# A two-layer transformer on one core: the first loads in another order and other pieces, with the order of work laid out anew

## The chip, the cores and the metric

The kernel runs on one core of a Trainium2 chip. The metric is device time of one execution in microseconds (us). The kernel before takes 2652.07 us, the median of three runs (2652.02 to 2653.28).

## The reference, cut to what matters

```python
def _A_ref(x, mem0, Wq, Wk, Wv, Wo, seg_len):       # x 2048 x 576; 32 heads of 128; memory of 8 rows
    mem = mem0
    for s in range(64):                             # segments of 32 rows, one after the other
        h = jnp.concatenate([mem, x[:, s * 32:(s + 1) * 32, :]], axis=1)        # 40 rows
        q, k, v = (jnp.einsum('btd,dhe->bhte', h, W) for W in (Wq, Wk, Wv))
        scores = jnp.einsum('bhqe,bhke->bhqk', q, k) * scale
        p = _softmax(jnp.where(mask[None, None], scores, -1000000000.0), axis=-1)
        o = jnp.einsum('bhte,hed->btd', jnp.einsum('bhqk,bhke->bhqe', p, v), Wo)
        mem = o[:, :8, :].copy()                    # the next segment needs this one's output
        outs.append(o[:, 8:, :])
def _B_ref(x, w1, w3, w2):                          # 576 -> 4608 -> 576
    return jnp.einsum('bsf,fd->bsd', _silu(x @ w1) * (x @ w3), w2)
x = x + _A_ref(_layernorm(x), ...); x = x + _B_ref(_layernorm(x), ...)
x = x + _A_ref(_layernorm(x), ...); x = x + _B_ref(_layernorm(x), ...)          # the same weights again
```

All inputs and weights are bf16. A segment depends on the one before it through `mem`.

## The kernel before, in words

The kernel walks through 72 steps. Step t works on segment t of the first attention layer and, from step 8 on, on segment t - 8 of the second one as well: steps 0 to 7 and the last eight have one layer, those between have two. Attention runs in a step by four groups of eight heads; the feed-forward part runs in jobs, one for every four steps, beside the attention of later steps.

The work is cut into nodes. `make_nodes` (L236) makes them with costs, dependencies and the pools they take room from; `plan` (L80) walks through them in the order of estimated times and lets each engine record its instructions in that order. Every engine keeps the order that the plan gives it. The order on TensorE is not found by the plan: it is written out by hand in three strings, `FIRST` (L205), `FOUR` (L214) and `LAST` (L218). `ORDER = FIRST + FOUR * 11 + LAST`, so `FIRST` is 16 steps, `FOUR` four steps that are walked through eleven times, and `LAST` the last twelve. One letter is one node:

- `Q`, `q`: queries and keys of four heads, the four full chunks of the 576 rows of Wq and Wk, and the remainder of 64 rows. A `Q` is 32 matmuls, a `q` eight. There are eight of each in a step.
- `S`: scores of a group; then VectorE and ScalarE make the softmax into tile `PB`. `T`: transposes of it on TensorE, in steps of one layer. In steps of two layers a transposing DMA takes `PB` to `PTS` instead (node TRD).
- `V v X x G g`: values, `P`: probabilities times values (it reads `PTS` and `V`), `O`, `o`: the product with Wo, full chunks and remainder.
- `F f`: w1 and w3 of 256 of the 4608 columns, `W w`: the product with w2 for the first and the second layer. `a b n m p`: transposes around the layernorms.

A node has a mode: which part of the array its matmuls use (whole, halves of columns, halves of rows). Some nodes can run whole or by halves; then `plan` takes what the nodes beside them have, and by halves such a node has twice the instructions (`Emitter.mm`). Which of ACT and DVE empties a bank is also the plan's choice (nodes "AD").

Loads: `em.dma` issues on SyncE's queue (SP), `em.adma` on ScalarE's (ACT), `em.swdma` on GpSimd's. Costs and due times of a load only set where it stands in its queue; on the chip an instruction waits for the data it reads or overwrites and, in the queue of a DMA, for one of eight semaphores that the DMAs of SP and ACT take in turn. Before, the loads go like this: SP has the 64-row remainder of Wq and half of that of Wv, then the first half of the heads of Wq in four pieces of 512 KB (one for each 128 rows) and of Wk in four, then the second half in eight, then Wv in four pieces of 1 MB, Wo in four groups, w1 and w3 of the first feed-forward nodes, w2, and x of the second 128 rows. ACT has the remainder of Wk, x of the first 128 rows, mem0, and the other half of Wv's remainder.

In step 0 the first `Q` of each half of the heads is preceded by twelve matmuls with no use of their result (L920 to L922), three behind each chunk of Wk as it lands:

```python
for c in range(4 if first and t == 0 and u % 4 == 0 else 0):
    for _ in range(3):
        self.mm(self.bk(b[1])[:], self.T.ident[:, 0:P], self.T.W[:, 4 + c, u * 512:(u + 1) * 512], True, True)
```

`first` is true if this `Q` stands ahead of the `q` of the same four heads. Ahead of everything, L1303 to L1321 fill constants: GpSimd does the masks, `HT` and `YTS`, VectorE `PB`, `V` and the eight banks.

Of the kernel before, what the change touches and what calls it, by code (L numbers as in the profile page):

```python
# [13 lines left out]
P = 128  # L14
R64 = 64
D = 576
# [183 lines left out]
def ewh(*ns):  # L200
# [5 lines left out]
    "maQQQqqqqQSQQTSqQQqSTqqSvVXxPPTOPOTOooPoOoQqqqqQQSQQSqvVQqQSqTQqXPSTOPTOaooPxTOPoOoQqqQQSQqqvVqSQqqQQqSTQPSTOPOT"  # L206
    "PTOPoooOoQqqqqQQSQvVSqqQQqqQQSTPTSXPOoTxPTOPOOoooQqqqpQQvVSqnQQqfSFQQqqqQSTFfTSPFOfPoTWPOFTOPfooOoFQQqqqfQSFfqqV"
    "vQWSQQFqfqTQSFWqfPQOTFPSfXWoTxfOPTFPOOoooFfqqQQFSQfqVvqqQWSQTFfqfFQQPSWTQfqqOPSFTOPFWTOPooffOooFQQqqqqQSQWVvSFfq"
    "QQTqWqqSQPTQaOSPbOTXPxooTOPxoOoXpqqQQqqQSQqvnQSfFQqVSfqFQfFPqQfFSPWfFPOoOOoofFPWOoFQQqfqfFSQqqqqQQQSWGSqqgQQFfgP"
    "GSWPGFfggfFGPOOWPOOooooFfqqQQQfSFqqQvFSWVfqqQQfFSWqQQqfPPSFOOFoPWOffFPaooOoWQqqqqQQSbQQSGgqqqQQgSPGqQOSPGOgGPgoO"  # L210
    "PooOoQqqqppQQQvSqqVnnSQFqqfQQFPSqffQFPOSoWwFFPffOOWPwOoooFqffqQQFwQQqqfSWGFSFqgqfQQQPQSWFqfqgGSwggGPGOPOOPWOFooo"
    "oFffqqQQQQqqawSSFfqqqQQQWvSwVffqFQFPPWSwFfOOPFWwffFPOOooooWQQqqqQSqqqQQQSbwGSgqqgQQPGSggGPGOPOOPoooOo"
)
FOUR = (  # L214
    "QqqqppQvVSQQnnQFfqqFSfqqQQFfqQSwPWPSFffOOWPFwFPOOooooFffqqQQwQQqqgSWGSFqqfQQQPQSWFqfqfFSwGgggGPGOPOPOOwoooFWoFff"
    "qqQQQQqqSFSqqfQQwWvVSQQFfqqfFSPWPOOwFffPFOWPwOooooFqqfQQqqaSQQWqSQQqqqQQSbwGSggGPGPggGPOOOPoooOo"
)
LAST = (  # L218
    "QpqqqQpQSvqqQQnSVqQnQFPSffqqFQOPSFOwPooffOFPWOooFqfqqQQQQfqSWwGSgqFQFPQwQqqfGSFfqgQOPSWggGGPOFPOOoWowooFfqfqQQQQ"
    "qqSWFSfqqQQwVvFSFfqqfQQPWOPSwFoOoffFPwPOOoWoFfqqqQQQQSWwqfFSFfqqQQWvvVSVqqPQQOSbwXPxPOOPoooOoQQpqqpVvqqQSQQqSnnQ"  # L220
    "QqqFTSffqFPTQOPSWFffTFPTOOPwOooooFfqqQQQSQQvqqqVwFWSfqfFqqQQQTSwWSFPTffOTPFOTPwPOOooooWFfqfqFQQQSQqqvxXVwWSFTFff"
    "qqQQQwqqSQTPWPffSFOTFPwTOPOWOooooFvfqqVQQWSFQqfqQwSFfqqQQqTSqWQPTQOTSPPoOObwTxoPXOooQQqqvpSQQqqVSnqQFfqQFTSQfqPQ"
    "qfTFSPOTwFPOOTFPffooOoowVqqqvQQQSQfqqFSQQqqqwQSTQPFTSOPXffOTFPTxOPwOooooFFqqffQQqqQSQQSqqVvqfQFTSQwPQqfTOSFPFTOf"
    "PwTOPFOfooooQQqqqQSvqqQVSqQTQSPQQqqTOSPFwTFffPOTOPoooOopwfFnFfffFFwFwfffFFFwffFFwfffFFwFwfffFFFwffFFwfffFFww"
# [11 lines left out]
def make_nodes(em, nseg, pools, o=Opt, dma_bw=230e3, load_bw=400e3):  # L236
# [26 lines left out]
    node("DMA", 4.0, lambda n: None, prio=-999.0, name="boot")  # L263
    ld_m0 = node("ACT", 0.6, em.load_m0(), prio=-90, name="m0", lat=8.0)
# [97 lines left out]
    def step(t):  # L362
# [17 lines left out]
        for g in range(NG):  # L380
            qs, qe = [], []
            for u in (2 * g, 2 * g + 1):
# [3 lines left out]
                m_ = node("PE", 32 * mm80, em.qk(t, u, b), deps=hx + hm[:1] + ([ld_h[u // 4]] if t == 0 else []),  # L386
                          prio=pq, mode="full", acq=[q] + b, name="QK")
                n = node("PE", 4 * mm80, em.qk_tail(t, u, b), deps=hx + hm + ([ld_h[u // 4]] if t == 0 else []), prio=pq + o.qkt, mode="row",
# [75 lines left out]

    last_up = []
    last_reads = [], []
    kept = {}

    def job(j):

# [113 lines left out]
class Emitter:  # L584
# [83 lines left out]
    def load_qk(self, half):  # L668
        def f(n):
            h = slice(half * 2048, (half + 1) * 2048)  # L670
# [690 lines left out]
```

## Time and profile before

| | before |
|---|---|
| median of three runs | 2652.07 us |
| the profiled execution / its span | 2657.81 us / 2656.0 us |
| busy: PE, DVE, ACT, POOL | 97%, 76%, 48%, 5% of the span |
| TensorE's granted clock, mean | 0.995 |
| instructions | 131716 |
| DMA | 373.13 MB, 140 GB/s in the mean |

The profiled execution's own time is 1.8 us over its span, and 5.7 us over the median. Lines name the place in the kernel file; nearly all matmuls have line L607 (`Emitter.ch` records them), so groups are told apart by their tiles and shapes. In a row of matmuls, 128*64 means that 128 rows and 64 columns of the array are in use.

### The profile page before, as it was taken

The numbers are of one execution on the slowest core, as the hardware profiler recorded it, in microseconds if no ns is written. First come the engines' busy times: TensorE is split into PE (matmuls) and PEld (weight loads), VectorE is DVE, ScalarE is ACT, GpSimd is POOL, SyncE is SP. The second block draws the span as 40 slices with busy tenths as digits, with TensorE's granted clock in tenths as the row PEclk, the third lists the DMA queues.
The fourth block names the chain that finished last, engine by engine and source line by source line (L and its number), as shares of the span: only waits on it lengthen the run. The fifth ranks groups of instructions, "written<-read, shape, count | busy, mean of one in ns | idle before, by whom it ended". The sixth has DMA issues, their size and how long they took to land.

```text
span 2656.0 us, 131716 instructions
## 1 busy us (share of the span) xinstructions
PE 2579.5 (97%) x58546; PEld 2209.3 (83%) x58546; DVE 2011.5 (76%) x5145; ACT 1265.5 (48%) x3744; POOL 128.8 (5%) x182
## 2 busy tenths in 40 slices
PE   6999999999999999999999999999999999999998
PEld 4788888788888878888888888888888888888886
DVE  4777786787787778778877777877777777777876
ACT  2655554444445444444545444454544445444552
POOL 1000000000000000000000000000000000000000
PEclk8999999999999999999999999999999999999999
DMA  9065745565555546446455654545465464545467
GB/s 322 4 181 136 185 105 145 121 154 133 126 143 112 148 118 157 131 130 146 114 142 114 157 133 128 147 111 140 117 158 147 119 155 93 142 120 148 118 172 247
DMA packets 686027, 373.13 MB, mean 140 GB/s; under 512 B 233897, under 2 KB 675633, under 8 KB 684817
## 3 DMA queue, kind: packets, MB, share of 16 engines
q1 hardware_dynamic: 681920, 356.84, 51.9%
q8 instruction: 457, 7.49, 1.2%
q0 software_dynamic: 3024, 6.93, 0.9%
q10 hardware_dynamic: 512, 0.94, 0.1%
q14 instruction: 114, 0.93, 0.1%
HBM read 308.49 MB, written 2.36 MB: 117 GB/s over the span
## 4 chain that ended last, share of the span: by engine, by line
PE 85%; DMA 8%; DVE 3%; issue 1%; SPq 1%; ACT 1%; POOL 0%; ACTq 0%; DVEq 0%; POOLq 0%
PE bank L607 85%; DMA PTS<-PB 5%; DMA W<-in_B_w_dram 2%; SPq L616 1%; DVE PB L613 1%; DMA W<-in_A_Wk_dram 1%; DMA W2C<-in_B_w_dram 1%; DVE STAT L613 0%; DVE SME L613 0%; DVE HTT L613 0%; DMA XN<-in_A_x_dram 0%; ACT V L610 0%; ACT HT L610 0%; DVE XR L613 0%; ACT SME L610 0%
## 5 line engine op out<-in xcount | busy, mean ns | idle before, releaser
L607 PEld LDWEIGHTS <-W 128*128 128x128 bf16 (+2 forms) x32064 | 1250.8, 100 | 129.4 <-issue 70.6
L607 PE MATMUL bank<-HT,W 128*128 128x80 bf16 (+3 forms) x23040 | 791.4, 197 | 13.9 <-issue 7.2
L607 PE MATMUL bank<-XTB,W 128*64 128x256 bf16 (+5 forms) x9024 | 662.5, 263 | 8.6 <-DMA W<-in_B_w_dram 5.5
L610 ACT ACTIVATE QKT<-bank 128x64 bf16<-128x64 f32 (+2 forms) x1645 | 377.4, 309 | 282.5 <-PE bank L607 270.8
L607 PE MATMUL bank<-OT,WO 128*128 128x80 bf16 (+2 forms) x11520 | 401.3, 198 | 3.7 <-issue 1.7
L610 ACT ACTIVATE V<-bank 32x512 bf16<-32x512 f32 (+1 forms) x577 | 324.9, 584 | 161.5 <-PE bank L607 155.4
L607 PEld LDWEIGHTS <-WO 128*128 128x128 bf16 (+1 forms) x11520 | 376.2, 102 | 24.9 <-issue 12.8
L607 PE MATMUL bank<-WV,HT 128*32 128x512 bf16 (+5 forms) x3592 | 366.7, 384 | 0.7 <-issue 0.7
L607 PE MATMUL bank<-W2C,HTT 128*64 128x288 bf16 (+1 forms) x3208 | 324.4, 287 | 1.0 <-DMA W2C<-in_B_w_dram 1.0
L613 DVE TENSOR_TENSOR PB<-SME,STAT 40x128 bf16<-40x128 f32 (+4 forms) x912 | 275.6, 336 | 40.0 <-DMA PTS<-PB 30.8
L610 ACT ACTIVATE HTT<-bank 128x512 bf16<-128x512 f32 (+1 forms) x324 | 175.0, 550 | 265.0 <-PE bank L607 263.1
L613 DVE TENSOR_REDUCE STAT<-SME 104x8 f32<-104x320 f32 (+1 forms) x576 | 275.2, 478 | 15.5 <-ACT SME L610 7.4
L613 DVE SCALAR_TENSOR_TENSOR XR<-bank,XR 128x288 f32<-128x288 f32 x576 | 240.5, 447 | 59.5 <-PE bank L607 54.7
L607 PEld LDWEIGHTS <-HT 128*32 128x32 bf16 (+5 forms) x3592 | 152.2, 99 | 145.8 <-issue 40.3
L610 ACT ACTIVATE OT<-bank 128x320 bf16<-128x320 f32 (+1 forms) x430 | 157.9, 403 | 229.4 <-PE bank L607 224.5
L613 DVE SCALAR_TENSOR_TENSOR HTT<-HTT,bank 128x512 bf16<-128x512 bf16 (+1 forms) x324 | 202.0, 624 | 80.0 <-ACT HTT L610 76.9
L607 PEld LDWEIGHTS <-HTT 128*64 128x64 bf16 (+1 forms) x3272 | 233.7, 105 | 30.9 <-issue 2.8
L613 DVE TENSOR_TENSOR HTT<-HTT,bank 128x512 bf16<-128x512 bf16 (+1 forms) x324 | 203.6, 628 | 29.5 <-PE bank L607 1.4
L610 ACT ACTIVATE SME<-SME 104x320 f32<-104x320 f32 (+1 forms) x288 | 135.6, 471 | 172.3 <-DVE SME L613 169.7
L613 DVE CAST V<-bank 64x512 bf16<-64x512 f32 (+1 forms) x287 | 196.1, 686 | 20.7 <-PE bank L607 14.8
L613 DVE CAST QKT<-bank 128x128 bf16<-128x128 f32 (+4 forms) x403 | 108.4, 316 | 100.0 <-PE bank L607 98.3
L613 DVE TENSOR_TENSOR SME<-bank,maskb 104x320 f32<-104x320 f32 (+1 forms) x288 | 138.4, 481 | 35.0 <-PE bank L607 29.1
(58 smaller groups left out, 1332.7 us busy)
## 6 DMA issues: line engine op xcount, KB each, us to landing
W<-in_B_w_dram SPq DMA_DIRECT2D x612, 256.0 KB, 3.6
W2C<-in_B_w_dram SPq DMA_DIRECT2D x306, 288.0 KB, 3.4
W<-in_B_w_dram SPq DMA_DIRECT2D x612, 32.0 KB, 3.5
W<-in_B_w_dram SPq DMA_DIRECT2D x8, 1024.0 KB, 13.6
W<-in_A_Wq_dram SPq DMA_DIRECT2D x9, 512.0 KB, 8.5
WO<-in_A_Wo_dram SPq DMA_DIRECT2D x4, 1152.0 KB, 16.7
XR<-in_A_x_dram POOLq DMA_DIRECT2D x16, 288.0 KB, 3.8
WV<-in_B_w_dram SPq DMA_DIRECT2D x4, 1152.0 KB, 10.0
```

The lines of the kernel that those rows point to most:

```text
L607: self.ch("PE", self.nc.tensor.matmul(out, lhsT=lhsT, rhs=rhs, start=start, stop=stop, skip_group_check=True, **k))
L610: self.ch("ACT", self.nc.scalar.activation(*a, **k))
L613: self.ch("DVE", getattr(self.nc.vector, fn_)(*a, **k))
L616: self.ch("SP", self.nc.sync.dma_start(out=out, in_=in_))
```

## The change

Loads: x of the first 128 rows and mem0 stand first, on ACT's queue; the four 64-row remainders (Wq, Wk, twice Wv) follow there. SP starts with Wq and Wk by quarters of the heads: 1 MB of Wq and 1 MB of Wk, four times, each one DMA over all four chunks of rows, with lines of 2 KB where they were 4 KB. The rest of SP's order stays, except that the first two w2 loads stand behind both of the first w1 and w3 loads. The nodes of these first feed-forward loads get a dependency on `WO2` of step 0 in the plan. In the built program that is only a place in the queue: these loads wait for semaphores of earlier DMAs there, and for none of TensorE's, before and after.

Useless matmuls: asked for ahead of `Q` 0, 2, 4 and 6 if they come ahead of their `q`, reading zeros in `V` and not the chunks of Wk. With the new string that is so for `Q` 6 alone: 24 such matmuls become 12.

Constants: `PB` and `V` are filled by GpSimd and not by VectorE.

Plan: other costs for the first loads, and all three strings are new, with the same letters in another order. The built programs have 58546 matmuls before and 58759 after, and 1198 and 1182 changes of mode.

```diff
-def make_nodes(em, nseg, pools, o=Opt, dma_bw=230e3, load_bw=400e3):
+def make_nodes(em, nseg, pools, o=Opt, dma_bw=230e3, load_bw=395e3):
...
-    ld_t = [load("ldt", 1.7 * kb(3 * R64, 4096), -10.0, em.load_tails(0)), node("ACT", 0.6, em.load_tails(1), prio=-120, name="ldt", lat=8.0)]
-    node("ACT", 0.6, em.load_tails(2), prio=-80, name="ldt", lat=10.0)
-    ld_h = [load("ldqk", kb(512, 4096), half - 9.0, em.load_qk(half)) for half in (0, 1)]
+    ld_t = [node("ACT", 0.6, em.load_tails(i), prio=-100 + i, name="ldt", lat=10.0) for i in range(4)]
+    ld_h = [load("ldqk", kb(1024, 1024) + (kb(3 * R64, 4096) if i == 0 else 0), i - 19.0, em.load_qk(i)) for i in range(4)]
...
+            ff_wait = [steps[0]["WO2"]] if j == 0 and pp == 0 else []
...
-                    ld = [node("DMA", kb(1152, 256) / dma_bw, em.load_w13(pr_, w13), prio=prio - 1, acq=[w13], lat=2.0, name="W13")]
+                    ld = [node("DMA", kb(1152, 256) / dma_bw, em.load_w13(pr_, w13), deps=ff_wait, prio=prio - 1, acq=[w13], lat=2.0, name="W13")]
...
+    def load_qk(self, i):
+        def f(n):
+            h = slice(i * 1024, (i + 1) * 1024)
             for kind, wd in ((0, self.a.wq), (1, self.a.wk)):
-                for c in range(4):
-                    self.dma(self.T.W[:, 4 * kind + c, h], wd[c * P:(c + 1) * P, h])
+                self.dma(self.T.W[:, 4 * kind:4 * kind + 4, h], wd[0:4 * P, h].rearrange("(c p) f -> p c f", p=P))
...
-            for c in range(4 if first and t == 0 and u % 4 == 0 else 0):
-                for _ in range(3):
-                    self.mm(self.bk(b[1])[:], self.T.ident[:, 0:P], self.T.W[:, 4 + c, u * 512:(u + 1) * 512], True, True)
+            for _ in range(12 if first and t == 0 and u % 2 == 0 else 0):
+                self.mm(self.bk(b[1])[:], self.T.ident[:, 0:P], self.T.V[:, 0, :], True, True)
...
-    nc.vector.memset(T.PB[:], 0.0)
-    nc.vector.memset(T.V[:], 0.0)
+    nc.gpsimd.memset(T.PB[:], 0.0)
+    nc.gpsimd.memset(T.V[:], 0.0)
```

The beginnings of the strings, which are step 0, and the second row of `FOUR`, in which steps 3 and 4 of the four lie:

```diff
-    "maQQQqqqqQSQQTSqQQqSTqqSvVXxPPTOPOTOooPoOo...
+    "amqQQqqqQQSqSqQQSTQQqqSTvVXxPTPOOPTOPoooOo...
...
-    "qqQQQQqqSFSqqfQQwWvVSQQFfqqfFSPWPOOwFffPFOWPwOooooFqqfQQqqaSQQWqqSQqqQQQSbwGSggGPGPggGPOOOPoooOo"
+    "QQFQQqqvwSSFfqqVQwQWFPSFffqqQQPOWSwFFPffOOWPwOooooFfqqQQqqaSQQWqqSQqqQQQbSwGSggGPGggPGPOOPoooOo"
```

More of the change, by code (lines that the diff above doesn't have):

```diff
@@ L205 @@
 FIRST = (
[L206 to L210, printed above, removed]
@@ L221 @@
[L221 to L224, printed above, removed]
+    "QpqqqQpQSvqqQVSQnQnQqqFSPffqQOPSoFFOPwOffFPWOoooFqqfQQQQqqfwSSFWqqQQGQfgqSFPFGgfqQOPSWwGggOPGWOPFOooowoFqqfQQQQq"
@@ L467, in make_nodes @@
     kept = {}
+    ff_wait = []
     def job(j):
@@ L543, in x_in @@
         xn = Slot("xn")
-        ld = node("DMA" if g else "ACT", 0.8 if g else 0.6, em.load_xn(g, xn), deps=reads_ht.get(4 * g - 3, [])[:1], prio=4 * g - 3.0 if g else -100, acq=[xn],
-                  name="ldxn", lat=2.5 if g else 9.0)
+        ld = node("DMA" if g else "ACT", 0.8 if g else 0.6, em.load_xn(g, xn), deps=reads_ht.get(4 * g - 3, [])[:1], prio=4 * g - 3.0 if g else -120, acq=[xn],
+                  name="ldxn", lat=2.5 if g else 4.5)
         ht_set(0, g, ln_nodes("L0", xn, xn, [ld], 4 * g - 2.0 if g else -8, ht_writes(0, g)))
```

47 lines of the change are left out of this document (26 added, 21 removed).

## The prediction

> **What bounds the kernel now.** The page comes first: the engines' shares and the chain that ended last.
>
> ```profile
> span 2656.0 us, 131716 instructions
> PE 2579.5 (97%) x58546; PEld 2209.3 (83%) x58546; DVE 2011.5 (76%) x5145; ACT 1265.5 (48%) x3744; POOL 128.8 (5%) x182
> PE 85%; DMA 8%; DVE 3%; issue 1%; SPq 1%; ACT 1%; POOL 0%; ACTq 0%; DVEq 0%; POOLq 0%
> ```
>
> TensorE is busy for 97% of the span and carries 85% of the chain. A load can be worth something only where TensorE waits for it. The table of stretches (busy us of each engine and count, granted clock, share of the DMA engines, GB/s) shows where that is.
>
> ```profile
> 0.00:10.00 10.00, 0.00 (x0) 0.00 (x0) 6.13 (x10) 0.00 (x0) 5.12 (x16) 1.00 0.79 191
> 20.00:30.00 10.00, 6.75 (x178) 5.02 (x177) 3.76 (x11) 1.47 (x5) 0.00 (x0) 1.00 1.03 408
> 40.00:50.00 10.00, 7.93 (x112) 3.43 (x112) 6.68 (x20) 2.88 (x7) 0.00 (x0) 0.66 1.07 385
> 50.00:60.00 10.00, 7.70 (x236) 7.17 (x237) 5.46 (x12) 6.21 (x17) 1.61 (x2) 0.83 1.07 342
> 60.00:70.00 10.00, 10.00 (x337) 8.28 (x334) 7.46 (x21) 5.36 (x14) 0.00 (x0) 1.00 0.04 10
> 100.00:110.00 10.00, 9.68 (x282) 8.03 (x280) 3.95 (x13) 3.07 (x10) 0.00 (x0) 0.71 0.01 3
> ```
>
> For the first 60 us the DMA engines are full and TensorE is not; from 60 us on it is the other way round. Step 0 is the place. When do its last weights land? For the last piece of Wk, of Wv and of Wo, the view of their tiles says when it was issued and how long it took.
>
> ```profile
> L616 SPq DMA_DIRECT2D W<-in_A_Wk_dram x1: 328/328/328, 21.3 to 21.3; - x1
> DMA to landing us min/median/max: 11.3/11.3/11.3
> L616 SPq DMA_DIRECT2D WV<-in_A_Wv_dram x1: 328/328/328, 26.5 to 26.5; - x1
> DMA to landing us min/median/max: 16.3/16.3/16.3
> L616 SPq DMA_DIRECT2D WO<-in_A_Wo_dram x1: 2873/2873/2873, 42.9 to 42.9; - x1
> DMA to landing us min/median/max: 11.8/11.8/11.8
> ```
>
> Wk is there at 32.6, Wv at 42.8, Wo at 54.7. The timeline of the same time, on POOL, ACT and PE:
>
> ```profile
> 5.57 0.30 POOL L1315 MEMSET maskb<- 8x40 bf16 x2
> 12.41 0.56 POOL L776 TENSOR_TENSOR LNS<-LNS,mhalf 128x1 f32<-128x1 f32 x1 [6.54 <-DVE LNS L613]
> 15.58 0.96 ACT L610 ACTIVATE HT<-bank 128x320 bf16<-128x320 bf16 x4
> 22.02 3.96 PE L607 MATMUL bank<-HT,W 128*128 128x40 bf16 x160
> 42.99 6.56 PE L607 MATMUL bank<-WV,HT 64*32 64x512 bf16 x80
> 55.85 0.96 POOL L1029 MEMSET PB<- 128x1024 bf16 x1 [42.87 <-PE bank L607]
> 57.66 1.55 PE L607 MATMUL bank<-OT,WO 128*64 128x40 bf16 x48
> 59.52 3.15 PE L607 MATMUL bank<-HT,W 128*128 128x40 bf16 x128 [0.32 <-ACT HT L610]
> ```
>
> The value products start at 42.99, with the last piece of Wv just in. The last products with Wo end at 57.66 + 1.55 = 59.2, 4.5 us behind the last piece of Wo; between them lies a chain through V, P and the evictions. Step 1 begins at 59.52.
>
> **x first, and the constants.** In the built order the two fills of `PB` and `V` stand on POOL ahead of the power of the first layernorm (L776). They begin where the masks end, 5.57 + 0.30 = 5.9; `PB`'s 1024 elements take 0.96, so `V`'s 4096 about 3.8: the power starts at about 10.6, not at 12.41, however early x lands. HT was complete 15.58 + 0.96 - 12.41 = 4.1 us behind it, so now at 14.7 instead of 16.5. This fill takes the place of the wait for x.
>
> **The loads.** The bytes up to Wo are the same, in the same sequence of matrices, and the queue never ran dry. What changes is the rate. The first two rows below have 64-row remainders alone, the third 4 KB lines over 128 rows; the last two, from the end of the span, have the 2 KB lines over 128 rows that the quarters will have.
>
> ```profile
> 3.00:6.00 3.00, 0.00 (x0) 0.00 (x0) 2.67 (x6) 0.00 (x0) 2.67 (x9) 1.00 1.02 238
> 6.00:8.00 2.00, 0.00 (x0) 0.00 (x0) 1.75 (x4) 0.00 (x0) 0.00 (x0) 1.00 0.97 197
> 18.00:30.00 12.00, 8.75 (x183) 5.64 (x182) 3.76 (x11) 1.47 (x5) 0.00 (x0) 1.00 1.03 408
> 2625.00:2629.00 4.00, 4.00 (x69) 3.54 (x67) 3.24 (x8) 1.23 (x4) 0.58 (x1) 1.00 1.05 402
> 2635.00:2639.00 4.00, 4.00 (x58) 3.33 (x56) 3.19 (x8) 0.63 (x2) 0.00 (x0) 1.00 1.04 384
> ```
>
> Wq and Wk are 8.39 MB: 20.6 us at 408, 21.3 at 393, the mean of the last two. So everything behind them lands 0.8 us later (0.3 to 1.3 by the two rows): Wk at 33.4, Wv at 43.6, Wo at 55.5. The remainders are 1.57 MB and take 7.2 us at 218 GB/s, the mean of their two rows, with the DMA engines 97% busy and more; on ACT's queue they use those same engines. The Trainium skill, "DMA: Bandwidth & Descriptors", section "Issuing engines are not separate DMA queues", speaks against this part of the change: DMAs of either issuer run on the same 16 engines, and a second issuer saves only the time of issuing. By that rule the remainders still cost their full time, and the trace agrees with its 0.97.
>
> The first quarter needs the remainders, x and 2.1 MB (5.3 us): data starts at about 1.7, so it lands at 1.7 + 7.2 + 0.4 + 5.3 = 14.6 and a little latency, say 16, and the first Q starts there and not at 22.0. That lead of 6 us is worth nothing: the fourth quarter is at 33.4 all the same. Behind it stand Q 6 and 7 (64 of 160 in 3.96: 1.6 us), four remainders, an eviction and scores, 3 us together. The twelve useless matmuls no longer wait for Wk and run in the 5 us between two quarters; if they stretch past the landing, by at most 2.6 us, the values' first three chunks still find themselves waiting for Wv at 43.6. That wait is their cover, of some 4 us.
>
> **The end of step 0.** Values: the last chunk's share is 6.56 / 4 = 1.6, so 45.2 instead of 49.6, and the chain behind it, 59.2 - 49.6 = 9.6 long, would end at 54.9. Wo ends later: 55.5 and then O 3 and o 3, 40 of 48 instructions of 1.55 us, 1.3: 56.8. What is late next, once the wait for x and Wv's late start are gone, is Wo. 59.2 - 56.8 = a gain of 2.4 us, between 0.4 (Wo 2 us later yet) and 2.9 (only 0.3 later). The dependency of the first feed-forward loads is worth nothing: they stand right behind Wo on SP before and after, and neither program has them wait for TensorE.
>
> **TensorE's other work.** The new strings move nodes between whole and half forms. Busy us by form:
>
> ```profile
> L607 PE MATMUL bank<-XTB,W 128*64 128x256 bf16 x4608 | 279.7, 273 | 0.0
> L607 PE MATMUL bank<-XTB,W 128*128 128x256 bf16 x1728 | 206.6, 273 | 0.0
> L607 PE MATMUL bank<-W2C,HTT 128*128 128x288 bf16 x1272 | 181.5, 287 | 1.0 <-DMA W2C<-in_B_w_dram 1.0
> L607 PE MATMUL bank<-W2C,HTT 128*64 128x288 bf16 x1936 | 143.0, 286 | 0.0
> L607 PE MATMUL bank<-WV,HT 128*128 128x512 bf16 x512 | 121.2, 380 | 0.0
> L607 PE MATMUL bank<-OT,WO 128*128 128x80 bf16 x7168 | 281.7, 202 | 1.4 <-DVE OT L613 1.1 <-ACT OT L610 0.3
> ```
>
> A pair of halves of w1 and w3 takes 279.7 / 2304 = 121.4 ns, a whole one 119.6; 256 more pairs make +0.5 us. For w2 147.7 against 142.7, 64 more pairs, +0.3. Transposes of XN and the P nodes go the other way, 55 and 48 pairs fewer; at w2's 5 ns -0.5. Together +0.3. There are 16 changes of mode fewer. Their price isn't a row; it is bounded by these:
>
> ```profile
> 1036.52 0.38 PE L607 MATMUL bank<-WV,HT 64*128 64x512 bf16 x2
> 1036.83 0.40 PE L607 MATMUL bank<-QKT 128*64 128x40 bf16 x15
> PEld L607 <- issue: 97.3, 343, 1.3
> ```
>
> The two remainders run side by side, 121.2 / 512 = 0.24 us, and the next mode starts 0.31 behind them: 0.07 for a change. From above, 97.3 / 343 = 0.28 for a wait of the weight load in 600 to 2260 us. I take 0.07, the nearer row: -1.1 (0 to -4.5).
>
> **Waits in the eleven rounds.** TensorE's largest wait in 600 to 2260 us is for the transposed probabilities:
>
> ```profile
> PE bank L607 <- DMA PTS<-PB: 10.2, 17, 1.2
> ```
>
> A round is about 155 us, so this is 10.7 rounds: 1 us a round, at 17 of the 171 groups. What decides is what stands on TensorE between `S` and `P` of a group. In `FOUR` three of 16 groups have short covers before; such a one is the third, `S W P w P S F f f O O W P`. The twelfth has `S P W P O O w F f f P F O W P`, and the new string makes that `S w F F P f f O O W P`: one F, an O and a W leave, and a small w's place moves. By the rows an F is 16 x 119.6 = 1.9 us, an O 32 x 39.3 = 1.26 and a W 8 x 142.7 = 1.14. The cover falls from about 13 to 9.8 us, the same as the third group's. The other groups near the limit keep theirs. Five groups a round carry the waits now (three short ones and two at ends of steps), 10.2 / 53 = 0.19 each; a sixth costs 11 x 0.19 = +2.1, with 0 and 11 x 1.2 = +13 as ends. `FIRST` and `LAST` are reordered in the same manner, with about as many short covers gained in the one as lost in the other; I take 0 for them.
>
> **The sum.** -2.4 + 0.3 - 1.1 + 2.1 = -1.1 us, so 2656.7 for the profiled execution (2657.81 before), which lay 5.7 over the median of the runs; for the median 2652.07 - 1.1 = 2651.0. What a measurement of this kernel can tell from no change is about 0.2%, 5.3 us, so this is no change.
>
> **The rivals.**
> 1. Slower: the twelfth group becomes a standing wait. Its place is the DMA from `PB` to `PTS`, of which there is one buffer of `PB`, so a late group holds the next one's softmax. From 0.8 us a round on it eats the rest and takes the time past 0.2% (11 x 0.8 = 8.8, and 8.8 - 3.2 = +5.6). At the longest wait seen, 1.2 a round, it is 13.2 - 3.2 = +10.0: 2662.1. For it speaks that the limit is near; against it that the third group, with the same cover, does not always wait.
> 2. Faster: the strings are better than I can see. In 100 to 110 us the clock was 0.71 behind a thin stretch; without that dip up to 2.9 us are saved, and changes of mode at 0.28 give -4.5: -2.9 - 4.5 - 2.4 + 0.3 = -9.5 without the twelfth group's waits, 2642.6. Half the modes' bound gives 2644.8.
> 3. The change doesn't do what it says: x first is held by POOL, and the first quarters' lead ends at Wo. If step 0 ends at 59.2 all the same, the sum is +1.3: 2653.4, in the same band.
> 4. The remainders on the second queue run beside the rest. At 408 they would take 3.9 us instead of 7.2: 3.3 more off all landings, so step 0 ends 3.3 earlier still, bounded by the values' chain at 54.9 - 3.3 only, and the sum is -4.4: 2647.7. The row with 0.97 speaks against it, and it stays under 0.2%.
>
> The Trainium skill, "TensorE: Matmul & The Clock Gate", Part 1, says an idle stretch over about 3.4 us drops the clock to a half. The 0.66 in 40 to 50 us agrees; as step 0 will end with Wo, it changes no term here.
>
> **How the numbers follow.** Forecast with rivals 3 and 4, which stay within 5.3 us: 0.62 (forecast 0.45, rival 3 0.11, rival 4 0.06). Rival 2: 0.22. Rival 1: 0.16. The range reaches from most of rival 2, 2643.5, to most of rival 1, 2659.0. Chances: faster 0.22, same 0.62, slower 0.16.
>
> **What would show it.** In the profile after: the power on POOL at 10.6 and not at x's landing; the first Q at about 16; the last pieces landing at 33.4, 43.6 and 55.5; step 1's Q at about 57.1; TensorE's wait for `PTS` a fifth more in the rounds, its longest under 1.5. Wrong would be: Wo landing before 53 or after 58, a step 1 that starts at 59 or later, or a round that is 0.5 us longer or shorter than now.

## The result, and the profile after

The changed kernel takes 2667.77 us (median of six, 2664.52 to 2672.56) against 2652.68 (2651.62 to 2659.97) of the kernel before beside it: a ratio of 1.0051 (95% interval 1.0035 to 1.0067), 15 us slower. Measured again on another chip, beside parts of the change (e14 below), it was 1.0028 (1.0019 to 1.0038), 7 us slower. The forecast was 1.1 us faster, and 2667.77 lies above its range. The profiled execution took 2669.58 us. Its page:

```profile
span 2667.8 us, 132116 instructions
PE 2580.1 (97%) x58729; PEld 2227.4 (83%) x58759; DVE 2014.4 (76%) x5191; ACT 1263.7 (47%) x3696; POOL 133.4 (5%) x184
PE 81%; DMA 10%; DVE 5%; issue 2%; SPq 1%; ACT 1%; POOL 0%; ACTq 0%; DVEq 0%; POOLq 0%
```

TensorE's busy time is the same (2579.5 before); its share of the chain fell from 85 to 81%, and DMA, VectorE and issue gained. So TensorE waits longer. The table of stretches of the changed kernel (columns as in the prediction):

```profile
20.00:30.00 10.00, 4.56 (x130) 4.12 (x129) 3.48 (x10) 1.08 (x3) 0.00 (x0) 1.00 1.05 387
40.00:50.00 10.00, 6.70 (x127) 3.71 (x128) 7.11 (x15) 5.64 (x13) 0.00 (x0) 0.88 1.05 390
50.00:60.00 10.00, 8.01 (x230) 7.67 (x227) 3.00 (x10) 2.77 (x9) 1.61 (x2) 0.50 1.11 358
```

Where the kernel before moved 408 GB/s from 20 to 30 us, this one moves 387. From 50 to 60 us TensorE runs wholly at half its clock (0.50, before 0.83). The last pieces of Wk, Wv and Wo (issue, and time to landing):

```profile
L617 SPq DMA_DIRECT2D W<-in_A_Wk_dram x1: 3047/3047/3047, 18.8 to 18.8; - x1
DMA to landing us min/median/max: 15.8/15.8/15.8
L617 SPq DMA_DIRECT2D WV<-in_A_Wv_dram x1: 635/635/635, 27.3 to 27.3; - x1
DMA to landing us min/median/max: 17.3/17.3/17.3
L617 SPq DMA_DIRECT2D WO<-in_A_Wo_dram x1: 2895/2895/2895, 44.7 to 44.7; - x1
DMA to landing us min/median/max: 11.8/11.8/11.8
```

They land at 34.6, 44.6 and 56.5 us, and in the kernel before at 32.6, 42.8 and 54.7: 1.8 to 2.0 us later now. The timeline of step 0, lines that answer to those of before:

```profile
10.42 0.56 POOL L775 TENSOR_TENSOR LNS<-LNS,mhalf 128x1 f32<-128x1 f32 x1
...
13.59 0.96 ACT L611 ACTIVATE HT<-bank 128x320 bf16<-128x320 bf16 x4
...
16.08 0.62 PE L608 MATMUL bank<-HT,W 128*128 128x40 bf16 x13 [1.42 <-DMA W<-in_A_Wk_dram]
...
44.68 1.39 PE L608 MATMUL bank<-WV,HT 128*32 128x512 bf16 x24 [0.86 <-DMA WV<-in_A_Wv_dram]
...
56.56 1.58 PE L608 MATMUL bank<-OT,WO 128*128 128x40 bf16 x40 [0.68 <-DMA WO<-in_A_Wo_dram]
58.47 3.71 PE L608 MATMUL bank<-HT,W 128*128 128x40 bf16 x124 [0.32 <-ACT HT L611]
```

Step 0 goes as forecast in kind: TensorE waits for Wv and then for Wo, and step 1 starts at 58.47 and not 59.52, 1.05 us earlier. The loss comes later. By the times at which the last `o` of each step ends, the changed kernel is 0.6 us behind the kernel before at the end of step 7 and 8.7 at the end of step 8; it is 3.8 behind after step 66, 9.1 after step 71 and 11.8 at the end of the span. These are differences of two single executions.

### The profile page after: what moved, and what is told of

Same layout as the page of the kernel before. It is cut to its first block, busy times and chain, and to the rows that moved or that the text cites. A ratio compares the mean times of both kernels' runs of the same rounds, so it can differ in the third digit from the quotient of the medians.

```text
span 2667.8 us, 132116 instructions
## 1 busy us (share of the span) xinstructions
PE 2580.1 (97%) x58729; PEld 2227.4 (83%) x58759; DVE 2014.4 (76%) x5191; ACT 1263.7 (47%) x3696; POOL 133.4 (5%) x184
## 4 chain that ended last, share of the span: by engine, by line
PE 81%; DMA 10%; DVE 5%; issue 2%; SPq 1%; ACT 1%; POOL 0%; ACTq 0%; DVEq 0%; POOLq 0%
PE bank L608 81%; DMA PTS<-PB 5%; DMA W<-in_B_w_dram 2%; SPq L617 1%; DVE PB L614 1%; DVE HTT L614 1%; DVE SME L614 1%; DVE STAT L614 1%; DMA W<-in_A_Wk_dram 1%; DMA W2C<-in_B_w_dram 1%; DMA WO<-in_A_Wo_dram 0%; DVE XR L614 0%; DMA W<-in_A_Wq_dram 0%; DVE V L614 0%; ACT HT L611 0%
## 5 line engine op out<-in xcount | busy, mean ns | idle before, releaser
L608 PEld LDWEIGHTS <-W 128*128 128x128 bf16 (+2 forms) x32320 | 1268.6, 101 | 146.3 <-issue 69.6
L608 PE MATMUL bank<-HT,W 128*128 128x80 bf16 (+3 forms) x23040 | 801.2, 197 | 24.8 <-ACT HT L611 8.0
L611 ACT ACTIVATE QKT<-bank 128x256 bf16<-128x256 f32 (+2 forms) x1647 | 380.6, 308 | 300.2 <-PE bank L608 272.9
L608 PE MATMUL bank<-OT,WO 128*128 128x80 bf16 (+3 forms) x11520 | 405.2, 199 | 2.6 <-DMA WO<-in_A_Wo_dram 1.7
L611 ACT ACTIVATE V<-bank 32x512 bf16<-32x512 f32 (+1 forms) x589 | 333.4, 585 | 128.4 <-PE bank L608 121.4
L608 PE MATMUL bank<-WV,HT 128*32 128x512 bf16 (+4 forms) x3580 | 361.0, 381 | 5.0 <-issue 3.5
L611 ACT ACTIVATE OT<-bank 128x320 bf16<-128x320 f32 (+1 forms) x406 | 151.8, 406 | 283.6 <-PE bank L608 280.6
L608 PEld LDWEIGHTS <-HT 128*32 128x32 bf16 (+4 forms) x3608 | 154.5, 99 | 135.1 <-issue 29.6
L614 DVE CAST V<-bank 64x512 bf16<-64x512 f32 (+1 forms) x275 | 188.4, 686 | 16.8 <-PE bank L608 11.5
L614 DVE CAST QKT<-bank 128x64 bf16<-128x64 f32 (+4 forms) x401 | 109.0, 317 | 91.4 <-PE bank L608 89.2
```

What stands on the lines that cost most here:

```text
L608: self.ch("PE", self.nc.tensor.matmul(out, lhsT=lhsT, rhs=rhs, start=start, stop=stop, skip_group_check=True, **k))
L611: self.ch("ACT", self.nc.scalar.activation(*a, **k))
L614: self.ch("DVE", getattr(self.nc.vector, fn_)(*a, **k))
```

## The experiments

The kernel before took 2652.8, 2651.7, 2645.7, 2645.2 and 2647.2 us beside the five groups below (e1 to e4, e6 to e9, e10 to e13, e14 to e17, and e18; each group on a chip of its own), so kernels are compared by their ratio to it. A difference of two ratios from different groups is weaker than one within a group, and the first measurement of the changed kernel, 1.0051, belongs to none of them. In the table "changed" is the changed kernel with one thing altered.

| kernel | median us | ratio, 95% interval |
|---|---|---|
| new loads, all strings old (e1) | 2648.1 | 0.9983, 0.9974 to 0.9991 |
| old loads, all strings new (e2) | 2656.1 | 1.0012, 1.0003 to 1.0020 |
| changed, FIRST old (e3) | 2655.5 | 1.0009, 1.0000 to 1.0018 |
| changed, LAST old (e4) | 2659.9 | 1.0019, 1.0009 to 1.0029 |
| changed, f20 later (e6) | 2660.2 | 1.0029, 1.0015 to 1.0044 |
| changed, wait filled (e7) | 2656.3 | 1.0022, 1.0010 to 1.0033 |
| new loads, FOUR new (e8) | 2653.6 | 1.0009, 0.9997 to 1.0020 |
| e1, fills on VectorE (e9) | 2647.8 | 0.9981, 0.9970 to 0.9991 |
| e8, twelfth S earlier (e10) | 2660.8 | 1.0054, 1.0042 to 1.0066 |
| e1, long lines (e11) | 2644.2 | 0.9993, 0.9983 to 1.0004 |
| changed, half of the last loads (e12) | 2644.7 | 1.0001, 0.9988 to 1.0014 |
| changed, last five steps old (e13) | 2646.5 | 0.9995, 0.9985 to 1.0006 |
| changed again (e14) | 2652.3 | 1.0028, 1.0019 to 1.0038 |
| new loads, FIRST new (e15) | 2647.8 | 1.0009, 0.9999 to 1.0020 |
| new loads, LAST new (e16) | 2643.0 | 0.9990, 0.9979 to 1.0001 |
| e1, step 0 filled (e17) | 2641.1 | 0.9983, 0.9973 to 0.9993 |
| changed, last loads nearly gone (e18) | 2643.4 | 0.9985, 0.9975 to 0.9995 |

**Loads or strings.** e1 is the changed code with the three strings of before (the twelve useless matmuls at Q 6 alone, as in the changed kernel):

```diff
-FIRST, FOUR, LAST of the changed kernel
+FIRST, FOUR, LAST of the kernel before
```

> The new loads, constants and plan costs with the three strings of before (the useless matmuls kept to Q 6, as the new kernel has them). Theory A, the loss comes from the strings: within 3 us of before (2652.7), step 0 ending about 1 us earlier. Theory B, the loss comes from the loads or from filling PB and V on GpSimd, or from what the plan makes of their costs later: about as slow as the changed kernel, 2664 to 2671.

e2 is the kernel before with the three new strings:

```diff
-FIRST, FOUR, LAST of the kernel before
+FIRST, FOUR, LAST of the changed kernel
```

> Before with the three new strings and nothing else (no useless matmul comes ahead of its q then, so there are none). Theory A: 10 to 17 us over before, 2663 to 2670, with the wait for w1 and w3 in step 8 and the half clock behind it. Theory B: within 3 us of before.

e3 is the changed kernel with one string exchanged:

```diff
-FIRST of the changed kernel
+FIRST of the kernel before
```

> The changed kernel with FIRST of before (useless matmuls at Q 6 alone), FOUR and LAST new. Theory A says that about 8 of the loss lie in step 8, which FIRST orders: 5 to 9 us under the changed kernel, about 2660. A rival that spreads the loss over the rounds: under 2 us from the changed kernel.

e4, likewise:

```diff
-LAST of the changed kernel
+LAST of the kernel before
```

> The changed kernel with LAST of before, FIRST and FOUR new. Theory A puts some 7 us of the loss into the last five steps and the end: 4 to 8 us under the changed kernel, about 2661. If FIRST alone is the cause: no change from it.

The new loads with the old strings are faster than the kernel before (e1). The changed kernel with an old FIRST or an old LAST lies below its first measurement, 1.0051 (e3, e4); against its second, 1.0028, only e3 does so clear of the intervals. So the loss lies in the strings. But with the old loads the same strings cost only 0.0012, 3 us (e2), where one theory wrote down 10 to 17 and the other less than 3 either way: they lose more beside the new loads. What the loads add to it is not known as a whole; in step 0 a part of it shows. Wo's last products and step 1's first `Q` in e2:

```profile
54.83 1.52 PE L607 MATMUL bank<-OT,WO 128*128 128x40 bf16 x40 [1.28 <-DMA WO<-in_A_Wo_dram]
56.67 3.49 PE L607 MATMUL bank<-HT,W 128*128 128x40 bf16 x124 [0.32 <-ACT HT L610]
```

With the loads of before and the new strings, and with no useless matmuls, step 1 starts at 56.67: 2.85 us earlier than in the kernel before, and 1.8 earlier than in the changed kernel. So the gain in step 0 can be had without the new loads, and beside the new strings they take 1.8 us of it back.

**Step 8.** The changed kernel's timeline there, its loads of `W` for the waiting node (issues, time to landing), and the timeline of the kernel before:

```profile
253.15 0.58 PE L608 MATMUL bank<-XTB,W 64*128 64x128 bf16 x4 [2.75 <-DMA W<-in_B_w_dram]
253.66 2.32 PE L608 MATMUL bank<-HT,W 128*128 128x80 bf16 x32
```

```profile
L617 SPq DMA_DIRECT2D W<-in_B_w_dram x4: 452/572/1042, 247.1 to 249.3; - x4
DMA to landing us min/median/max: 3.2/3.7/4.9
```

```profile
250.03 1.31 PE L607 MATMUL bank<-HT,W 128*128 128x80 bf16 x32
251.27 1.39 PE L607 MATMUL bank<-XTB,W 64*128 64x128 bf16 x20
```

The four matmuls at 253.15 are `f20`, the third remainder of the second feed-forward job. Its weights were issued at 247.1 to 249.3 and landed 3 to 5 us later, and the new string has `f20` ahead of `Q` 70 where the old one has it behind. TensorE stands 2.75 us. The next 32 `Q` matmuls then take 2.32 us where the kernel before takes 1.31. The stretch behind the wait, first of the changed kernel and then of the kernel before:

```profile
252.00:259.00 7.00, 5.85 (x80) 5.34 (x81) 2.54 (x8) 2.39 (x7) 0.00 (x0) 0.52 0.41 112
```

```profile
252.00:259.00 7.00, 6.28 (x155) 5.28 (x153) 5.95 (x16) 4.36 (x15) 0.00 (x0) 1.00 1.01 219
```

A clock of 0.52 and 80 matmuls, against 1.00 and 155. The Trainium skill, "TensorE: Matmul & The Clock Gate", Part 1, gives an idle window of about 3.4 us for this, free-running against the program. As the length of one wait that figure differs here: 2.75 us were enough, and at the same four matmuls 2.21 us in e12 and 1.86 us in e4 (0.76 in the stretch in both). By the trace's record of the clock the half rate began at 252.33, within the wait, and lasted 6.83 us; in the second profile of the changed kernel (e14) the wait was 2.73 us and the half rate lasted 3.41 us (0.81 in the stretch). That the window runs free fits this, and so does a wait of 2.79 us in e6, below, with a clock of 1.00 behind it; no run shows it directly.

e6 puts `f20` and `F20` behind the four nodes of Q 70 and 71:

```diff
-F f f Q F P q q Q F f
+F f Q q q Q f F P F f
```

> The changed kernel, with one place of FIRST altered: the third feed-forward remainder of the second job (f20) and its F20 stand behind Q 70, q 70, q 71 and Q 71 of step 8 and not ahead of them. By the theory that the loss is local (a remainder placed ahead of the landing of its weights, and the half clock after the wait), TensorE's wait of 2.75 us at 250.4 falls below 0.5 us and the half-clock stretch at 252.3 goes: 5 to 9 us less than the changed kernel's 2667.8, so 2659 to 2663. By the rival that the new loads and the new strings lose together wherever the nodes stand, the wait turns up elsewhere and the time stays within 3 us of 2667.8.

The half clock went (1.00 in 252 to 259), and of `f20`'s wait 0.23 us were left. But a `P` now waits 2.8 us for `PTS` in the same step, and step 8 takes 38.8 us; it took 42.9 in the changed kernel (40.1 in e14) and 34.8 before. The cause of `f20`'s wait was right; of the 8.1 us that the step had lost, 4.1 are won back, and the new wait holds 2.8 of the rest. The ratio, 1.0029, lies under 1.0051 and at 1.0028, so the time alone doesn't tell it from the changed kernel.

e7 leaves the order and fills the wait:

```diff
 first = self.begin(b)
+for _ in range(12 if first and tail and pr == 2 and not last and list(ents) == [(0, 1)] else 0):
+    self.mm(self.bk(b[1])[:], self.T.ident[:, 0:P], self.T.W[:, 0, 0:512], True, True)
```

> The changed kernel with twelve useless matmuls of 512 columns ahead of f20 (about 2.8 us by 0.24 us each), so that TensorE is busy while it waits for the weights; the order is the changed kernel's. If the half clock behind the wait is a price of its own, the wait stays and the half-clock stretch at 252.3 (6.8 us, in which 3.4 us of work are lost) goes: about 2664. If only the wait counts: 2667.8 as before. If useless matmuls only delay f20: above 2668.

`f20` starts 2.5 us behind the nodes ahead of it, about as long as the wait was, but the stretch behind it has its full clock:

```profile
252.00:259.00 7.00, 6.80 (x172) 6.17 (x171) 3.95 (x13) 3.21 (x12) 0.00 (x0) 1.00 0.86 189
```

172 matmuls where the changed kernel did 80. Step 8 takes 37.0 us, 5.9 less than in the changed kernel's first profile and 3.1 less than in its second (e14). The waits for `W2C` later in the step, 2.2 us in the first profile, are gone here too; the other 3.7 are put down to the clock. So the clock has a price beside the wait, and in the first profile a larger one. By the ratio, 1.0022, e7 is faster than the first measurement, but not clear of the second.

e15 has FIRST alone new:

```diff
-FIRST of the kernel before
+FIRST of the changed kernel
```

> New loads with FIRST alone new, FOUR and LAST of before. The new loads with all strings of before had a ratio of 0.9983. By the two stretches that FIRST showed (the wait for the third remainder's weights with the half clock behind it 8 us, and one or two half clocks ahead of it), 6 to 12 us more: 1.0005 to 1.003. If FIRST loses only together with the other strings: 0.997 to 0.9995.

```profile
251.29 0.46 PE L608 MATMUL bank<-XTB,W 64*128 64x128 bf16 x4 [3.20 <-DMA W<-in_B_w_dram]
```

The wait is there, 3.20 us, without the other strings, and the ratio is 0.0026 over e1's and e17's (e17, below, is of the same chip): 6.9 us of 2648, with some 4 us to each side. In every profile with the new FIRST and neither of the two mends (e6, e7), the granted clock fell to between 0.52 and 0.81 behind this place; in none with the old FIRST did it. Step 8 takes 38.2 to 42.9 us in the first kind and 34.8 to 37.0 in the second.

**FOUR.** e8 is e1 with one string exchanged:

```diff
-FOUR of the kernel before
+FOUR of the changed kernel
```

> The new loads, with FOUR new and FIRST and LAST of before (the kernel of the first experiment with FOUR alone exchanged; that took 2648.1). By the differences of the runs so far FOUR is worth nothing: 2647 to 2650. By the term of the prediction for the twelfth group's cover it is +2.1 less 0.8 for the modes, about 2649.4. By the rival in which the twelfth group becomes a standing wait, 2656 or more.

TensorE's waits for the transposed probabilities in 600 to 2260 us, of e1, of e8 and of the changed kernel:

```profile
PE bank L608 <- DMA PTS<-PB: 5.7, 10, 1.0
```

```profile
PE bank L608 <- DMA PTS<-PB: 9.1, 14, 1.3
```

```profile
PE bank L608 <- DMA PTS<-PB: 10.1, 16, 1.3
```

By the first two FOUR costs 3.4 us more of this wait. Not every profile says so: with the new loads the old FOUR has 4.3 to 5.8 us of it and the new one 5.2 to 10.8, and the kernel before, with the old FOUR, has 10.2. By time FOUR is 0.0026 to 0.0028 over e1 and e9 (6.9 to 7.4 us), with some 4 us to each side. Summing the idle time ahead of the twelfth group's eleven `P` gives 1.2 us in e8 and 1.0 to 3.1 in the other profiles with this group as the new string has it (e2, 1.1, among them), less than 0.3 in each of those with the new loads and the old FOUR, and 1.0 in the profile before. So the twelfth group is a part of what FOUR costs, and the rest is not found.

e10 gives that group a longer cover by an earlier `S`:

```diff
-QQPOWSwFFPffOOWP
+QQPSOWwFFPffOOWP
```

> The kernel with FOUR alone new (2653.6), with the twelfth group's S two nodes earlier: P S O W w F F P f f O O W P where the new string has P O W S w F F P f f O O W P. Its cover between S and P grows from about 9.8 to 12.2 us. If the twelfth group is what FOUR pays for, its waits in the eleven rounds (1.2 us in the profile of that kernel, 1.1 to 3.1 in the others with the new FOUR, none with the old) go, and 1 to 3 us of time with them: 2651 to 2653. If the loss of FOUR lies in other groups, 2653 to 2655; if S itself now waits for the evictions of its Q, 2655 or more.

```profile
PE bank L608 <- ACT QKT L611: 11.2, 11, 1.0
PE bank L608 <- DMA PTS<-PB: 9.9, 13, 1.9
```

The twelfth group's wait went, but `S` now comes ahead of the evictions that it reads and waits 1.0 us in each of the eleven rounds. The price is 0.0045 over e8 (another chip), 12 us, of which the row of `QKT` explains 11.2: the third branch of what was expected. The `O` and `W` ahead of `S` were the cover of the evictions.

**The loads.** e9 is e1 with the fills on VectorE again:

```diff
-nc.gpsimd.memset(T.PB[:], 0.0)
-nc.gpsimd.memset(T.V[:], 0.0)
+nc.vector.memset(T.PB[:], 0.0)
+nc.vector.memset(T.V[:], 0.0)
```

> The kernel of the first experiment (new loads, old strings, 2648.1) with the fills of PB and V on VectorE again, as before the change. The first layernorm's power should start on GpSimd at about 7 and not at 10.4. If the gain of the loads lies in the order and the pieces of the loads, nothing follows, because the first Q waits for Wk until 16: 2647 to 2650. If the gain of 4.7 us lies in the fills on GpSimd: 2652 to 2653.

The power of the first layernorm starts at 9.17 (7 was expected); the time stays (0.9981 against 0.9983). The fills are worth nothing either way.

e11 is e1 with pieces and lines of before:

```diff
-h = slice(i * 1024, (i + 1) * 1024)
-for kind, wd in ((0, self.a.wq), (1, self.a.wk)):
-    self.dma(self.T.W[:, 4 * kind:4 * kind + 4, h], ...)
+h = slice(i * 1024, (i + 2) * 1024)
+for kind, wd in ((0, self.a.wq), (1, self.a.wk)) if i % 2 == 0 else ():
+    for c in range(4):
+        self.dma(self.T.W[:, 4 * kind + c, h], wd[c * P:(c + 1) * P, h])
```

> The kernel of the first experiment (new loads, old strings, 2648.1), with Wq and Wk by halves of the heads in pieces of 512 KB with lines of 4 KB, as before the change; x first, the remainders on ScalarE's queue and the fills stay. If the lines of 2 KB make the landings late, Wk lands at 33.4 or earlier (34.5 with quarters) and Wo at 55.5 or earlier (56.5), and step 0 ends 1 us or more earlier: about 2647. If the remainders beside the rest make them late, the landings stay within 0.3 us and the time with them. The first Q starts later, at about 22, which is worth nothing.

Wo's last piece, and TensorE at the end of step 0:

```profile
L617 SPq DMA_DIRECT2D WO<-in_A_Wo_dram x1: 2884/2884/2884, 45.0 to 45.0; - x1
DMA to landing us min/median/max: 11.9/11.9/11.9
```

```profile
37.91 3.09 PE L608 MATMUL bank<-V,ident 128*128 128x512 bf16 x12
...
45.27 5.95 PE L608 MATMUL bank<-WV,HT 64*32 64x512 bf16 x80
...
61.27 0.90 PE L608 MATMUL bank<-HT,W 128*128 128x40 bf16 x30 [0.32 <-ACT HT L611]
```

With lines of 4 KB Wo lands at 56.9, no earlier than with 2 KB (e1: 56.6). The stretches of 8 to 16 and 16 to 22 us, of the kernel before and of the changed kernel, show one reason for the late landings:

```profile
8.00:16.00 8.00, 1.00 (x10) 0.76 (x11) 2.38 (x10) 1.70 (x4) 0.56 (x1) 1.00 1.05 347
16.00:22.00 6.00, 4.12 (x12) 1.39 (x12) 0.00 (x0) 0.54 (x4) 0.00 (x0) 1.00 1.03 411
```

```profile
8.00:16.00 8.00, 1.51 (x22) 1.14 (x22) 1.29 (x6) 2.24 (x5) 2.90 (x2) 1.00 1.02 254
16.00:22.00 6.00, 3.01 (x88) 2.73 (x88) 0.65 (x2) 0.61 (x2) 0.00 (x0) 1.00 1.07 353
```

The remainders, the last of which lands at 19.2, run beside the quarters, and until then the rate is lower; the DMA engines are full in all four rows. From 2 to 8 us it is the other way round (219 GB/s before, 312 now), but summed up to 22 us the changed kernel has moved 0.5 MB less, which is 1.2 us at 408 GB/s. The next ten us, without remainders, of e1 and of e11:

```profile
22.00:32.00 10.00, 6.58 (x188) 6.13 (x188) 3.91 (x12) 1.91 (x6) 0.00 (x0) 1.00 1.05 387
22.00:32.00 10.00, 5.90 (x167) 5.41 (x167) 3.64 (x11) 1.47 (x5) 0.00 (x0) 0.99 1.03 408
```

Lines of 2 KB move 387 GB/s here (386 in the changed kernel), lines of 4 KB 408 (414 in the kernel before): 28 GB/s less over 10 us is 0.7 us. So the lines delay the landings too, by about as much as was forecast, and the first 22 us, with the remainders beside the quarters, by more; 1.2 + 0.7 is the 1.8 to 2.0 measured. In e11 the better rate only makes up for 0.3 MB less than e1 moved by 22 us, for which the traces show no reason.

e11 starts step 1 at 61.27, 2.7 us later than e1: the values start at 45.27, behind the useless matmuls and the last `Q`, and not behind Wv. With the old strings and these useless matmuls the quarters' lead keeps step 0 with its loads; e2, with neither, does without the lead. By the ratio e11 is 2.6 us behind e1, inside the intervals.

e17 is e1 with waits of step 0 filled:

```diff
 # P of group 0 in step 0: six; transposes of group 3 in step 0: five
+for _ in range(n):
+    self.mm(self.bk(b[0])[:], self.T.ident[:, 0:P], self.T.W[:, 0, 0:512], True, True)
```

> New loads, strings of before, with eleven useless matmuls more in step 0: six ahead of the first P, which waits 1.6 us for V, and five ahead of the last transposes, behind which TensorE waits for Wo. They fill idle time only. If the half clock of 48.2 to 61.9 us in step 0 is a price of its own, it goes or is cut, and step 1 starts 1 to 2 us earlier than at 58.6 and runs at the full clock from its start: 1 to 3 us less, a ratio of 0.997 to 0.998. By the prediction's rule, that the clock changes no term because step 0 ends with Wo: no difference, 0.9983.

Step 1's first `Q` in e1 and in e17:

```profile
58.56 0.63 PE L608 MATMUL bank<-HT,W 128*128 128x40 bf16 x14 [0.32 <-ACT HT L611]
```

```profile
58.17 3.16 PE L608 MATMUL bank<-HT,W 128*128 128x40 bf16 x128 [0.32 <-ACT HT L611]
```

The clock from 57 to 62 us is 1.00 instead of 0.52, and step 1 ends 0.8 us earlier; the ratio is e1's. Under a wait for a load the half clock cost nearly nothing here.

**LAST.** e16 is e1 with one string exchanged:

```diff
-LAST of the kernel before
+LAST of the changed kernel
```

> New loads with LAST alone new, FIRST and FOUR of before. By the profiles so far (3.7 us more in the last five steps, 2.0 more behind them, 1.9 less ahead of them) 3 to 5 us more than with all strings of before: 0.9994 to 1.0002. By the difference of the medians with LAST exchanged in the changed kernel (7.9) 1.0013; by the last call (15) 1.004.

e13 sets back a part of that string in the changed kernel:

```diff
-LAST of the changed kernel from step 67 on
+LAST of the kernel before from step 67 on
```

> The changed kernel with LAST of before from step 67 on, new ahead of it. If LAST loses in its last five steps and behind them, all of its 7.9 us come back, as with the whole of LAST of before: 2659 to 2662. If it loses ahead of step 67: 2666 to 2668.

LAST alone costs 0.0007 (1.9 us, not outside the intervals). By the changed kernel and e4 it is 0.0032 with the first measurement and 0.0009 with the second, near e16's. With the last five steps of LAST set back the changed kernel comes to 0.9995. That is less than with all of LAST set back (e4, 1.0019), on another chip, so its size isn't LAST's price. The profiles of the changed kernel and the kernel before place the loss in the last five steps and behind them: 3.8 us behind after step 66, 11.8 at the end. What TensorE waits for there (from 2440 us on; first the changed kernel, then e1):

```profile
PE bank L608 <- issue: 7.5, 6, 2.6
```

```profile
PE bank L608 <- issue: 5.6, 4, 2.4
```

Every profile with the last steps of the new LAST and all the loads has 6.4 to 7.9 us of it, those with the old ones 3.5 to 6.0. The changed kernel's timeline between two such waits, and its instruction queue on the page:

```profile
2596.53 0.79 PE L608 MATMUL bank<-HT,W 128*128 128x40 bf16 x25 [0.85 <-issue]
2597.25 0.41 PE L608 MATMUL bank<-WV,HT 64*32 64x512 bf16 x8
2597.59 0.47 PE L608 MATMUL bank<-HT,W 64*128 64x40 bf16 x24
2597.99 1.91 PE L608 MATMUL bank<-WV,HT 128*32 128x512 bf16 x32
2599.83 0.37 PE L608 MATMUL bank<-QKT 128*40 128x40 bf16 x8
2600.14 0.94 PE L608 MATMUL bank<-HT,W 64*128 64x40 bf16 x31
2603.01 0.39 PE L608 MATMUL bank<-HT,W 128*128 128x40 bf16 x9 [1.93 <-issue]
```

```profile
q8 instruction: 459, 7.52, 1.2%
```

25 + 8 + 24 + 32 + 8 + 31 = 128 matmuls, with 128 weight loads: 256 instructions from one wait to the next. And 58759 of each fill 459 blocks of 256, as many as the packets of the instruction queue. In each kernel these waits stand at one count of matmuls modulo 128, give or take one (31 or 32 in the changed kernel, 25 or 26 in e16, 26 or 27 in e1). The Trainium skill, "Runtime: NRT & Kernel Launch", section "Instruction fetch mechanics", says that instructions come by DMA in blocks of 256 and that the cost of a boundary is mostly hidden. The blocks agree; hidden they are not, where the last job's loads fill the DMA engines (0.90 of them busy from 2580 to 2612 us) and 128 short matmuls are done in 5 us.

e12 and e18 take those loads away, in half and nearly wholly:

```diff
-self.dma(t13[:, 4 * kind:4 * kind + 4], wd[0:4 * P, ...])
-self.dma(t2, self.a.w2[fa:fa + 1024, :]...)
+self.dma(t13[:, 4 * kind:4 * kind + 2], wd[0:2 * P, ...])      # e12; in e18 the line is gone
+self.dma(t2[:, 0:4], self.a.w2[fa:fa + 512, :]...)             # e12; in e18 t2[:, 0:1] and 128 rows
```

> The changed kernel, with half the bytes of the last feed-forward job's loads left out (two of the four chunks of w1 and w3, half of w2), so that the DMA engines are full for about half as long in the last 80 us; the products run on what lies in the tiles. If TensorE's waits for nothing that the profile shows (7.5 us in six in the last steps) come from those full DMA engines, they fall to about 4 us, the half-clock stretches at 2604 and 2610 become fewer, and the wait for w1 and w3 at 2652 goes: 4 to 8 us less, 2660 to 2664. If they belong to the order of instructions: within 2 us of 2667.8 except for that last wait, about 2665.

> The changed kernel without the last feed-forward job's large loads: the full chunks of w1 and w3 and seven eighths of w2 are left out, the products run on what lies in the tiles. TensorE's waits for nothing that the profile shows, 6.5 to 7.9 us in the last steps of every kernel with the new LAST, stand 128 matmuls and 128 weight loads (256 instructions) apart, at one count of matmuls modulo 128 in each kernel, and the instruction queue moves about one piece of 16 KB for each 256 of TensorE's instructions. If they are instructions that come late because these loads fill the DMA engines, they go: under 1.5 us in the last 200 us, where half the loads left 5.1, and no half clock around 2600. If the order of nodes makes them, they stay above 5.

```profile
PE bank L608 <- issue: 2.0, 5, 0.8
```

With half the loads 5.1 us of the wait were left, in four; without them (the row, e18) 2.0, none over 0.9, a little more than the 1.5 written down. So most of these waits come from the last job's loads. The old order has such waits too, 1 to 2 us less of them on the same chip; that the new one moves more blocks of short matmuls into the time when the engines are full is an argument that no run tests. The ratios of e12 and e18, 1.0001 and 0.9985, are not the price of these waits alone, for other waits for the same loads go with them: 3.1 us for `W` in the changed kernel's first profile, from 2440 us on.

**The size.** e14 is the changed kernel unaltered.

> The changed kernel again, unaltered, beside the parts below on one chip: the kernel before took 2652 to 2653 us in four calls out of five and 2645.7 in the last one, and there two variants of the changed kernel lay 13 and 15 us closer to it than the changed kernel had. If the loss is of the size first measured, the ratio to the kernel before is 1.0035 to 1.0067 (2662 to 2671 where the kernel before takes 2652.7). If the size hangs on how fast the transfers of a chip are, less: 1.000 to 1.003.

1.0028: between the two branches, half of the first measurement, with intervals that just touch. Beside e1's 0.9983, FIRST (0.0026) and LAST (0.0007) make 1.0016, and with FOUR's 0.0026 to 0.0028, measured on another chip, 1.0042 to 1.0044: between the two measurements of the whole. The profiled execution here was the fastest of eleven (2641.49 us) and had 5.2 us of waits for `PTS` in 600 to 2260 us, against 10.1 in the first profile. From the end of step 15 to the end of step 59, where FOUR is at work, it took 1682 us, and the three profiles with the old FOUR on that chip (e15, e16, e17) 1684 to 1686; on the chip of e1 the old FOUR took 1687 and the new one 1692 to 1695 (e2, e3, e4). So FOUR's share does not show in the second measurement's profile. That the change is slower holds on both chips; by how much, between 0.2 and 0.7%, and whether it is the chip, stays open.

## Why the prediction was wrong

**The failed step** is "I take 0 for them", for the reordered FIRST and LAST. The argument counted short covers between `S` and `P`. It did not ask, for nodes with weights that come by DMA, whether a node was moved ahead of the landing. One letter in FIRST was: 2.75 us of waiting and a half clock behind it, 3 to 8 us in step 8, and 6.9 us by the ratio for FIRST alone (e15). For LAST, 1.9 us (e16) are inside the intervals; its profiles show more waits for instructions that come late.

**The clock** "changes no term here" held for step 0 (e17: 0.4 us at the start of step 1, 0.8 at its end), where the next thing is a load. It failed in step 8, where TensorE itself is the bound. The rule of the Trainium skill ("TensorE: Matmul & The Clock Gate", Part 1), read as one wait of 3.4 us, hid that 2.75 and less can suffice. The kernel before had shown it: its 0.66 in 40 to 50 us was said to agree, but TensorE's longest wait between 36 and 43 us there is 1.09 us, and its waits of over 0.15 us in that time sum to 2.6.

**The end of step 0**, -2.4, was -1.05: inside its bounds of 0.4 to 2.9. The power (10.42 for 10.6), HT (14.55 for 14.7) and the first Q (16.08 for 16) came as written. Wo landed at 56.5 and not 55.5, the term that was mis-sized by 1.0; the last 40 products took 1.58 and not 1.3, at half clock. The reason given for the delay, lines of 2 KB, holds for about 0.7 us of it (0.8 was forecast, at 393 GB/s; 386 were measured). What was missed is the 1.2 us by 22 us: the working let the remainders cost the same beside the quarters as ahead of them. Each half of the change moves the start of step 1 by itself: the strings beside the old loads by 2.85 (e2), the loads beside the old strings by 1.0 (e1), both together by 1.05. "That lead of 6 us is worth nothing" holds in e2 and not in e11, where step 0 ends 2.7 us later without it.

**The twelfth group**, +2.1, was 1.0 to 3.1 us of idle time ahead of its `P`, and 1.0 in the kernel before already. The wait is where it was forecast; that it grew by 2.1 the profiles don't show, for TensorE's wait for `PTS` in the rounds was 10.1 us after 10.2, not a fifth more. The nodes that leave its cover were misread as well: by the strings they are two `P`, an `O` and a `W`, and no `F`; the cover of 9.8 fits that. By time FOUR cost 6.9 to 7.4 us (e8), with some 4 to each side, where the working has about 1.3 for all of its terms. Rival 1, a standing wait of 10 us, did not come with this change; it came in e10, by the softmax's other neighbour, the evictions ahead of `S`. In e8 other groups of FOUR wait a little more as well, which the prediction had ruled out.

**Rivals 2 to 4** did not come as such. Rival 4's remainders run beside the rest, but at the cost of the rest. **Forms and modes** (+0.3 and -1.1): TensorE's busy time rose by 0.6, of the size forecast; what fewer modes brought wasn't measured by itself.

**The new loads** beside the old strings are worth about 0.0017 to 0.0019 (e1, e9, e17), 4 to 5 us. Step 0 shows 1.0 of it (step 1 starts at 58.56 in e1); the rest wasn't found, since the profiled execution before lay 5.7 us over its median and had 10.2 us of waits for `PTS` where e1 and e9 have 5.7. Beside the new strings they lose: 1.0012 without them (e2), 1.0028 and 1.0051 with them. The version that beats both kernels is the new loads with the old strings.

## What to carry to other kernels

When the order of an engine's work is rewritten, go through every moved node and ask when its last operand lands, transfers first; counting covers of one kind is not enough. A wait on an engine that is the bound costs the wait and can cost a slower clock behind it, so a useless matmul in the wait can pay, while under a load that ends later anyway it brings next to nothing. Measure the two halves of a change alone and together: here the loads help beside one order and hurt beside the other. Where a kernel fills the DMA engines to the brim, keep the stretch free of many short instructions, for the instructions come by the same engines.

## What the runs showed of the hardware

- One wait of 1.86 to 3.20 us on TensorE was followed by a half clock for 3.41 or 6.83 us (0.52 to 0.81 over the 7 us at this place, in the profiles with the new FIRST); 2.79 us in e6 were not (1.00). Filled with matmuls, the same 2.5 us were not either.
- TensorE's instructions arrive in blocks of 256, and blocks came up to 2.6 us late in the changed kernel (4.1 in e6) where the DMA engines were 90% busy and more; with the loads gone, none was over 0.9 us late.
- Lines of 2 KB over 128 rows moved 386 and 387 GB/s from 22 to 32 us, lines of 4 KB 408 and 414. With remainders over 64 rows beside the quarters the whole moved 353 GB/s from 16 to 22 us, where pieces over 128 rows alone moved 411 (the kernel before).
